# Retention followed by a four-expert feed-forward: one attention visit per chunk in place of three

## The chip, the cores and the metric

The kernel runs on one core of a Trainium2 chip, written in Bass with a Tile layer that places the buffers and their waits; the order of the instructions is the kernel's own. The metric is the device time of one execution in microseconds (us). Engines are called PE (TensorE; its weight loads are a row of their own, PEld), DVE (VectorE), ACT (ScalarE), POOL (GpSimd) and SP (SyncE, which here only issues DMAs).

## The reference, cut to what matters

```python
scores = np.matmul(q, k.transpose(0, 1, 3, 2)) / np.sqrt(64)     # batch 8, heads 8, seq 576, dim 64
ret = scores * Dmat              # Dmat = gamma_h ** (i - j) for i >= j, else 0
x = np.matmul(ret, v)            # -> 4608 tokens x 512
p = domain_probs / (domain_probs.sum(-1, keepdims=True) + 1e-09)
for e in range(4):
    out += p[:, e:e + 1] * (np.maximum(x @ w1[e], 0) @ w2[e])    # 512 -> 1024 -> 512
```

There is no softmax, so a chunk of 128 positions needs its own masked scores and one 64x64 state per head, summed over the chunks before it.

## The kernel before, in words

**The two parts.** Attention makes the token tiles `xT` (512 tokens each, nine of them); the experts turn a tile into 512 x 512 outputs. The weight products run as Strassen's seven in place of eight (`up_fast`, L650, and `Down`, L594), after a classical start (`up_classical`, `downs`, L490 and L512) that lasts until sums of weights and tokens are ready (`weight_sums`, `token_sums`, `down_sums`).

**Stages.** The main loop (L950) goes over pairs of tile and expert, a stage. Each stage has two half-stages g = 0 and 1, one call of `up_fast` each. A half-stage issues four fills (`fill(1)` to `fill(4)`, L971), in each of which the down products of the stage before are put between the up products. In the fast form the PE order of a half-stage is P R V V P Q W V P R W P V W, each letter being four matmuls of 256 columns into the PSUM bank of that name: `upP`, `upQ`, `upR`, `downV`, `downW`. P is written four times. Before the third writing DVE must have read the second (L675), before the fourth DVE must have read the third (L683). Bank Q is read for the last time by ACT at L677, before `fill(2)` ends, and is not used again until ACT copies P into it at L669 in the next half-stage.

**Attention between them.** Batches 0 and 1 are done in the head of the program, batches 2 to 7 by `Chain` (L738). Of a batch there are four chunks of 128 and a remainder of 64. Of each chunk PE has three pieces: `S` (scores, 8 matmuls of 64 rows, L328), `kv` (states, 8 matmuls of 64 columns, L339) and `O` (8 matmuls of 64 columns at L369, and from the second chunk on 4 full ones with the states before it, L372). They go to PSUM banks of the ring `at` (a0, a1, a2). DVE masks the scores (`mask`, L333, two of them) and sums the states (`kv_sum`), POOL copies the states to `sbd` (L362), ACT or DVE copies `O` into `xT` (L242). POOL also multiplies and casts the loaded q, k, v (L279, L281), and SP transposes q and k by DMA (L297). `Chain` keeps a list per engine; `emit` gives out the next entry when the numbers of entries done on other engines are reached. After every fill `between` (L960) offers PE one entry; `sums` and `window` give DVE and ACT theirs. So a batch has 14 PE entries, each between two full products.

**The head.** `plan` and `at(g, ...)` (L846) put small work behind the g-th group of the classical start. Behind groups 26 to 33 stand the sums of w1 of expert 2, behind 51 to 54 the `down_sums` of w2 of expert 1 (L562 to L565). Their result `dsum` lies in the buffer `w2s_1`, which before that holds the loaded k, q, v of chunk 1 of batch 1 (`raw_units`, L92): tags `w2s_0` to `w2s_3` serve as raw buffers for four chunks first. The remainder of batch 1 is transposed by PE (`Trem`, L315).

Of the kernel before, what the change touches and what calls it, by code (L numbers as in the profile page):

```python
# [23 lines left out]
def kernel(  # L24
# [10 lines left out]
    nc = tc.nc  # L35
# [215 lines left out]
    class Att:  # L251
# [111 lines left out]

        def O(self, c):
            st = self.sT[c]
            o = self.o = bank("at", [128, NP, C], FP32, "oc")
            for p in range(NP):
                for j in range(2):
                    nc.tensor.matmul(o[64 * j:64 * j + 64, p, :], lhsT=self.mc("v", c)[:, 2 * p + j, :],  # L369
                                     rhs=st[:, j, p, :], start=(p == 0), stop=False, skip_group_check=True)  # L370
            for p in range(NP if c else 0):
                nc.tensor.matmul(o[:, p, :], lhsT=sbd[:, c - 1, p, :], rhs=self.qc(0, c)[:, p],  # L372
                                 start=False, stop=(p == NP - 1), skip_group_check=True)
# [9 lines left out]
        def Srem_mask(self):  # L383
            st = self.sT["r"] = att2.tile([128, NP, R], BF16, tag="sT", name="sTr")
            nc.vector.tensor_tensor(st, self.srem, trir[:, :].unsqueeze(1).to_broadcast([128, NP, R]), op=MULT)
# [208 lines left out]
    class Down:  # L594
# [7 lines left out]

        def product(self, i):
            hT, h, w, t = hTs[self.nt, self.e], hsum[self.nt, self.e], w2_sb[self.e], dsum[self.e]
            lo, hi, a, b = slice(0, 4), slice(4, 8), slice(0, HD), slice(HD, Dm)
            if i == 1:
                self.V, self.W = (one_bank(x, [128, 2, HD], FP32, "down" + y) for x, y in zip(self.tags, "VW"))
            o, l, r = {1: (self.V[:, 0], hT[:, lo, :HT], w[:, lo, a]),
                       2: (self.V[:, 0], hT[:, hi, :HT], w[:, hi, a]),
                       3: (self.V[:, 1], h.get(4), w[:, hi, b]),  # L610
                       4: (self.W[:, 0], hT[:, hi, HT:], t[:, 2]),
                       5: (self.V[:, 1], h.get(1), t[:, 0]),
                       6: (self.W[:, 0], h.get(2), t[:, 1]),
                       7: (self.W[:, 0], hT[:, lo, HT:], w[:, lo, b])}[i]
            for k in range(NFC // 2):
                nc.tensor.matmul(o, lhsT=l[:, k, self.s * 128:(self.s + 1) * 128], rhs=r[:, k],  # L616
                                 start=(i == 1 and k == 0), stop=(k == NFC // 2 - 1), skip_group_check=True)
# [17 lines left out]
        def out(self, i, halves=(slice(0, 2),)):  # L635
            ns = 2 * i + self.s
            t, po = self.nt * NSUB + ns, (self.V, self.W)[i]
            pe = probs[:, self.e, t:t + 1]
            for x in halves:
                cols = slice(x.start * HD, x.stop * HD)  # L640
                a, src = acc[self.nt][ns][:, cols], po[:, x].rearrange("p a d -> p (a d)")
                if self.e == 0:
                    nc.scalar.activation(a, src, Copy, scale=pe)
                else:
                    nc.vector.scalar_tensor_tensor(a, src, pe, a, op0=MULT, op1=ADD)  # L645
                if self.e == E - 1:
                    eng = nc.scalar if len(halves) == 1 and x.start else nc.sync
                    eng.dma_start(out=out[t * 128:(t + 1) * 128, cols], in_=a)
# [87 lines left out]


    class Chain:  # L738
        def __init__(self):
            self.todo = {k: [] for k in ("PE", "DVE", "ACT", "POOL")}  # L740
            self.done = dict.fromkeys(self.todo, 0)
            self.seen = dict(self.done)
            self.now, self.begun, self.tokens = 0, {}, 2 * S
            for b in range(2, B):
                self.batch(b)

        def batch(self, b):
            A, n = Att.__new__(Att), b - 2
            P, V, X = 14 * n, 13 * n, 5 * n

            def add(kind, f, **need):
                self.todo[kind].append((f, need))

# [11 lines left out]

            g = nc.gpsimd
            for c in range(NCH):
                free = {"PE": P - 14 + (7 if c < 2 else 13)} if n else {}
                if c == 3:
                    free = {"PE": P + 2}  # L770
                if c == 0:
                    add("POOL", lambda: (begin(), cast(A.cast, "k", 0, g)), **free)
                else:
                    add("POOL", lambda c=c: cast(A.cast, "k", c, g), **free)
                add("POOL", lambda c=c: cast(A.cast, "q", c, g))
                add("POOL", lambda c=c: (cast(A.cast, "v", c, g), transposes(c)))
            add("POOL", lambda: cast(A.cast_rem, "k", g), **({"PE": P} if n else {"first": 1}))
            add("POOL", lambda: cast(A.cast_rem, "q", g))
            add("POOL", lambda: (cast(A.cast_rem, "v", g), transposes(NCH)))
            add("POOL", lambda: A.put_krem(g, A.qr[:, 1]), later=(b, NCH))  # L780

            def tokens(c):
                A.x(c, nc.scalar)
                self.tokens = b * S + min((c + 1) * C, S)

            def O(c, v, x):
                add("PE", lambda: A.O(c), DVE=V + v, ACT=X + x)

            def Sc(c, v, x):
                add("PE", lambda: A.S(c), DVE=V + v, ACT=X + x, later=(b, c), **({} if n else {"first": 2}))  # L790

            def kv(c, v, x=0):
                add("PE", lambda: A.kv(c), DVE=V + v, ACT=X + x)

            Sc(0, 0, -1 if n else 0), kv(0, 0), Sc(1, 2, 0), O(0, 3, 0), kv(1, 4), Sc(2, 5, 1), O(1, 6, 0), kv(2, 7)
            Sc(3, 8, 2), O(2, 9, 0), kv(3, 10)
            add("PE", A_(A, "Srem"), DVE=V + 11, later=(b, "r"))
            O(3, 11, 3)
            add("PE", A_(A, "Orem"), DVE=V + 13)
            for c in range(NCH):  # L800
                for j in range(2):
                    add("DVE", lambda c=c, j=j: A.mask(c, j), PE=P + (1, 3, 6, 9)[c])
                add("DVE", lambda c=c: A.kv_sum(c), PE=P + (2, 5, 8, 11)[c])
            add("DVE", A_(A, "Srem_mask"), PE=P + 12)
            for c in range(NCH + 1):
                add("ACT", lambda c=c: tokens(c), PE=P + (4, 7, 10, 13, 14)[c], tile=(b * S + min((c + 1) * C, S) - 1) // NT)

        def emit(self, kind, nt, strict=True):
# [4 lines left out]
            for k, n in need.items():  # L813
                if k == "later":
# [3 lines left out]
                    else:  # L818
                        ok = (b, c) in self.begun and (not strict or self.now >= self.begun[b, c] + 5)
                elif k == "first":  # L820
                    ok = len(rem1) < n
                elif k == "tile":
# [47 lines left out]
    def rem1_casts():  # L870
        for n in "kqv":
            a1().cast_rem(n, nc.gpsimd)
            loads["cast"] += 1
            load_ahead(len(PIECES))

    def a1():
# [16 lines left out]
    def narrow():  # L893
# [5 lines left out]
    at(48, narrow, lambda: state.update(t1=token_sums(1)), lambda: [f() for f in state["t1"][:3]])  # L899
    rem1 = {3: lambda: a1().Trem(), 5: lambda: (a1().Srem(), a1().Srem_mask()),  # L900
            7: lambda: (a1().Orem(), a1().x(NCH, nc.vector))}

# [7 lines left out]
    s0 = sums_at(weight_sums, 0, 20, 21, 22)  # L910
    sums_at(weight_sums, 2, 26, 28, 30, 33)
    sums_at(weight_sums, 3, 36, 38, 49, 50)
    sums_at(down_sums, 1, 51, 52, 53, 54)
    for g in range(49, 56):
        at(g, lambda: pool(1, 1))
# [19 lines left out]
    owed = [((1, 1), (2, 0), s0[3])]  # L935
    for e in (2, 3, 0):

# [12 lines left out]
    for nt, e in [(nt, e) for nt in range(1, n_nt) for e in range(E)][1:]:  # L950
# [9 lines left out]
        def between(i):  # L960
# [3 lines left out]
            if i == 3:  # L964
                pool(nt, 4 if gaps < 8 else 3 - g)
            rem1.pop(gaps, int)()
            chain.emit("PE", nt)
            chain.seen.update(chain.done)
            chain.now += 1

        def fill(i):  # L971
            if not fast:
                for _ in range(4):
# [9 lines left out]
            elif i == 2:  # L983
                d().product(6)
                d().copy("U")
                d().product(2)
            elif i == 3:
                d().product(7)
                d().add(12)
# [11 lines left out]
        def sums(i):  # L1001
# [3 lines left out]
            turns = {(0, 1): 0 if old else 2, (0, 2): 0 if old else 1, (0, 3): 1,  # L1005
                     (1, 1): 2, (1, 2): 1, (1, 3): 0 if new else 1}[g, i]
            if g == 0 and old:
# [5 lines left out]
            for _ in range(turns):  # L1013
                window("DVE")

        def window(kind):
# [7 lines left out]
        while nt not in tsum:  # L1024
            tokens(nt)
            if nt not in tsum:
                moved = [chain.emit(k, nt, strict=False) for k in ("POOL", "PE", "DVE", "ACT")]
                assert any(moved), (nt, chain.done, {k: v[:1] for k, v in chain.todo.items()})
        while front and e == 0:
            front.pop(0)()  # L1030
# [52 lines left out]
```

## Time and profile before

| | |
|---|---|
| median of 4 executions | 529.15 us (528.67 to 529.77) |
| profiled execution | 529.77 us, of which its span is 528.06 us |
| PE busy | 515.3 us, 98% of the span, 4878 matmuls |
| DVE, ACT, POOL busy | 397.4, 303.4, 180.7 us |
| granted PE clock, mean | 0.998 |
| longest idle times ended by a release, PE | 1.6 us in all, twice, waiting for DVE L675 |

Busy time of an engine counts its instructions and not what they hide. Because matmuls overlap, PE's rows are best read by their starts: from the start of one group of four matmuls to the start of the next is what that group costs PE.

### The profile page before, as it was taken

Reading aid. Unit: us, or ns where it says so; the run is one execution under the profiler, and the core shown is the slowest. Engines: PE = TensorE matmul, PEld = TensorE weight load, DVE = VectorE, ACT = ScalarE, POOL = GpSimd, SP = SyncE. Lnnn points to the kernel's source line nnn. Section 1 sums busy time; section 2 is a strip of 40 time slices with the busy share of each in tenths; the row PEclk is TensorE's granted clock in tenths of the full one; section 3 lists DMA queues with packets and bytes.
Section 4 is the critical chain, followed back from the end, with each engine's and each line's share of the span. In section 5 each row is a group of like instructions: output and inputs, shape, how many; then the busy total and the mean of one; then the engine's idle time right before and its main releaser. Section 6 shows DMA issues by size and latency. Waiting matters only on the chain.

```text
span 528.1 us, 12528 instructions
## 1 busy us (share of the span) xinstructions
PE 515.3 (98%) x4878; PEld 400.3 (76%) x4894; DVE 397.4 (75%) x736; ACT 303.4 (57%) x624; POOL 180.7 (34%) x273
## 2 busy tenths in 40 slices
PE   8999999899999999999999999999999999999995
PEld 3644455588666888888888888888888888888884
DVE  5624568888765898788878897788688976886675
ACT  3462254466346555755576666665765666666661
POOL 6702275253433244524424243333424121000010
PEclk9999999999999999999999999999999999999999
DMA  9999999752554239722764149241652110011002
GB/s 236 188 206 202 205 188 201 149 109 45 125 134 102 59 81 151 161 51 46 154 113 101 31 88 215 60 82 25 179 110 42 47 44 1 2 41 41 1 2 80
DMA packets 149260, 54.11 MB, mean 102 GB/s; under 512 B 130732, under 2 KB 144044, under 8 KB 149200
## 3 DMA queue, kind: packets, MB, share of 16 engines
q1 hardware_dynamic: 141872, 44.92, 39.4%
q0 software_dynamic: 7328, 8.39, 9.4%
q8 instruction: 38, 0.62, 0.5%
q14 instruction: 22, 0.18, 0.1%
HBM read 45.16 MB, written 9.44 MB: 103 GB/s over the span
## 4 chain that ended last, share of the span: by engine, by line
PE 92%; DVE 4%; issue 2%; DMA 1%; POOLq 0%; POOL 0%; SPq 0%; DVEq 0%
PE upP L663 21%; PE downV L616 18%; PE downW L616 14%; PE upR L663 10%; PE po L534 9%; PE ph L493 7%; PE upQ L663 5%; PE s L328 2%; PE oc L369 2%; PE kvp L339 1%; PE oc L372 1%; DVE acc L645 1%; DMA raw<-in_q_dram 1%; PE warm_out L164 1%; DVE qm L413 0%
## 5 line engine op out<-in xcount | busy, mean ns | idle before, releaser
L684 POOL TENSOR_SCALAR hT<-hT 128x512 bf16<-128x512 bf16 x62 | 38.3, 618 | 251.0 <-DVE hT L683 248.1
L663 PEld LDWEIGHTS <-wt 128*128 128x128 bf16 x992 | 92.6, 97 | 20.5 <-issue 3.0
L616 PEld LDWEIGHTS <-hT 128*128 128x128 bf16 x928 | 90.8, 98 | 11.4 <-issue 0.8
L663 PEld LDWEIGHTS <-wsum 128*128 128x128 bf16 x744 | 71.1, 98 | 10.0 <-issue 0.7
L663 PE MATMUL upP<-xT,wt 128*128 128x256 bf16 x496 | 74.6, 273 | 1.6 <-DVE upR L675 1.6
L616 PEld LDWEIGHTS <-hsum 128*128 128x128 bf16 x696 | 68.1, 98 | 8.2 <-issue 0.2
L675 DVE TENSOR_TENSOR upR<-upP,m 128x512 f32<-128x512 f32 x62 | 43.3, 698 | 40.9 <-PE upP L663 19.6
L616 PE MATMUL downV<-wt,hT 128*128 128x256 bf16 x464 | 69.3, 273 | 0.4 <-DVE acc L645 0.4
L669 ACT ACTIVATE upQ<-upP 128x512 f32<-128x512 f32 x62 | 36.2, 585 | 45.4 <-PE upP L663 45.3
L686 ACT ACTIVATE hT<-upR 128x512 bf16<-128x512 f32 x62 | 37.0, 597 | 38.6 <-PE upR L663 38.6
L677 ACT ACTIVATE hT<-upQ 128x512 bf16<-128x512 f32 x62 | 37.0, 597 | 32.9 <-PE upQ L663 31.7
L691 ACT ACTIVATE hT<-upP 128x512 bf16<-128x512 f32 x62 | 37.0, 597 | 31.8 <-DVE downW L633 16.0
L534 PE MATMUL po<-wt,hT 128*128 128x512 bf16 x213 | 51.9, 379 | 0.6
L683 DVE TENSOR_TENSOR hT<-upP,m 128x512 bf16<-128x512 f32 x62 | 42.7, 689 | 12.2 <-PE upP L663 9.8
L333 DVE TENSOR_TENSOR sT<-s,tri 128x512 bf16<-128x512 f32 x56 | 37.1, 681 | 5.8 <-PE s L328 5.8
L509 ACT ACTIVATE hT<-ph 128x512 bf16<-128x512 f32 x40 | 23.5, 597 | 29.1 <-PE ph L493 28.2
L663 PE MATMUL upR<-tsum,wsum 128*128 128x256 bf16 x248 | 37.2, 273 | 0.5 <-DVE tsum L562 0.5
L663 PE MATMUL upP<-tsum,wt 128*128 128x256 bf16 x248 | 37.2, 272 | 0.3 <-DVE hT L683 0.3
L663 PE MATMUL upP<-tsum,wsum 128*128 128x256 bf16 x248 | 37.4, 273 | 0.0
L663 PE MATMUL upR<-xT,wsum 128*128 128x256 bf16 x248 | 37.2, 273 | 0.0
L663 PE MATMUL upQ<-xT,wt 128*128 128x256 bf16 x248 | 37.2, 273 | 0.0
L586 DVE TENSOR_TENSOR hsum<-hT 128x512 bf16<-128x512 bf16 x58 | 33.9, 585 | 4.3 <-POOL hT L684 1.2
(134 smaller groups left out, 940.1 us busy)
## 6 DMA issues: line engine op xcount, KB each, us to landing
out_dram<-acc SPq DMA_DIRECT2D x32, 256.0 KB, 2.6
wt<-in_moe_w_dram POOLq DMA_DIRECT2D x6, 1024.0 KB, 25.3
raw_k<-in_k_dram SPq DMA_DIRECT2D x24, 256.0 KB, 3.8
raw_q<-in_q_dram SPq DMA_DIRECT2D x24, 256.0 KB, 3.4
raw_v<-in_v_dram SPq DMA_DIRECT2D x24, 256.0 KB, 3.8
raw<-in_k_dram SPq DMA_DIRECT2D x8, 256.0 KB, 5.7
raw<-in_q_dram SPq DMA_DIRECT2D x8, 256.0 KB, 5.8
raw<-in_v_dram SPq DMA_DIRECT2D x8, 256.0 KB, 5.6
```

The costliest lines, as they stand in the source:

```text
L333: nc.vector.tensor_tensor(self.sT[c][:, j], self.s[c][j], tri[:, :].unsqueeze(1).to_broadcast([128, NP, C]), op=MULT)
L493: nc.tensor.matmul(ph[:, ts], lhsT=w1_sb[e][:, dc, fc * 128:(fc + 1) * 128], rhs=xts[nt][:, dc, ts], start=(dc == 0), stop=(dc == NDC - 1))
L534: nc.tensor.matmul(po, lhsT=hT[:, fc, ns * 128:(ns + 1) * 128], rhs=w2_sb[e][:, fc, d:d + w], start=(fc == 0), stop=(fc == NFC - 1))
L616: nc.tensor.matmul(o, lhsT=l[:, k, self.s * 128:(self.s + 1) * 128], rhs=r[:, k], start=(i == 1 and k == 0), stop=(k == NFC // 2 - 1), ski ...
L663: nc.tensor.matmul(ps[:, l], lhsT=wa(kc)[:, f:f + 128], rhs=xa(kc), start=(start and l == 0 and kc == 0), stop=(kc == 1), skip_group_check ...
L669: nc.scalar.activation(Q, P, Copy)
L675: nc.vector.tensor_tensor(R_, P, m5, op=ADD)
L677: nc.scalar.activation(hT[:, lo, t0], Q, Relu)
L683: nc.vector.tensor_tensor(h22, P, m5, op=ADD)
L684: nc.gpsimd.tensor_scalar(h22, h22, float("inf"), 0.0, op0=MIN, op1=MAX)
L686: nc.scalar.activation(hT[:, lo, t1], R_, Relu)
L691: nc.scalar.activation(hT[:, hi, t0], P, Relu)
```

## The change

Scores of chunk c+1, states of chunk c and output of chunk c become one PE entry, `visit`. It stands only behind `fill(3)` (the entries of a batch's first chunk and its remainder also elsewhere). `O` goes to bank Q, and its copy to `xT` is put at the beginning of `fill(4)` (`put_late`). Of product 2 of `Down` (`downV`) three matmuls stay in front of the third P and one moves behind R, so that the PE order becomes P R V V P Q W V(3) P R V(1) W P V W. The outputs of expert 0 are half moved from ACT to DVE. In the head the `down_sums` of expert 1 go from groups 51 to 54 up to 32 to 35, those of expert 2 take their place, and the last w1 sum of expert 2 goes from 33 to 31. The remainder of batch 1 is transposed by DMA, and its masked scores take the place of its transposed k. The DMA transposes of a chunk are issued behind the cast of q, not behind that of v.

```diff
-        def O(self, c):
+        def O(self, c, tag=None):
             st = self.sT[c]
-            o = self.o = bank("at", [128, NP, C], FP32, "oc")
+            o = self.o = one_bank(tag, [128, NP, C], FP32, "oc") if tag else bank("at", [128, NP, C], FP32, "oc")
...
-            st = self.sT["r"] = att2.tile([128, NP, R], BF16, tag="sT", name="sTr")
+            st = self.sT["r"] = self.qr[:, 1]
...
-        def product(self, i):
+        def product(self, i, part=slice(0, NFC // 2)):
...
-            for k in range(NFC // 2):
+            for k in range(NFC // 2)[part]:
...
-                if self.e == 0:
+                if self.e == 0 and i == 1:
                     nc.scalar.activation(a, src, Copy, scale=pe)
+                elif self.e == 0:
+                    nc.vector.tensor_scalar_mul(a, src, pe)
...
-                add("POOL", lambda c=c: cast(A.cast, "q", c, g))
-                add("POOL", lambda c=c: (cast(A.cast, "v", c, g), transposes(c)))
+                add("POOL", lambda c=c: (cast(A.cast, "q", c, g), transposes(c)))
+                add("POOL", lambda c=c: cast(A.cast, "v", c, g))
...
+        def visit(self, A, b, c, last):
+            add, all_ = self.add, self.all
+            L, l = (A, c - 1) if c else (last, NCH - 1)
+            lb = b if c else b - 1
+            new = A is not None
+            def run():
+                if new:
+                    A.S(c)
+                if L:
+                    L.kv(l)
+                    L.O(l, "Q")
+                    self.late.append(lambda: self.put(L, lb, l))
...
+            if L:
+                add("DVE", lambda: L.kv_sum(l), **done)
+            for j in range(2 if new else 0):
+                add("DVE", lambda j=j: A.mask(c, j), **done)
+            if c == 0:
+                M = L or Later("a1")
+                add("PE", lambda: M.Srem(), DVE=all_["DVE"], later=(lb, "r"), any=1)
+                add("DVE", lambda: M.Srem_mask(), PE=all_["PE"])
+                add("PE", lambda: M.Orem(), DVE=all_["DVE"], any=1)
+                add("ACT", lambda: self.put(M, lb, NCH), PE=all_["PE"], tile=(lb * S + S - 1) // NT)
...
             a1().cast_rem(n, nc.gpsimd)
...
+        a1().dmaT(NCH)
...
-    sums_at(weight_sums, 2, 26, 28, 30, 33)
+    sums_at(weight_sums, 2, 26, 28, 30, 31)
+    sums_at(down_sums, 1, 32, 33, 34, 35)
     sums_at(weight_sums, 3, 36, 38, 49, 50)
-    sums_at(down_sums, 1, 51, 52, 53, 54)
-    for g in range(49, 56):
+    sums_at(down_sums, 2, 51, 52, 53, 54)
+    at(50, lambda: a1().put_krem(nc.gpsimd, a1().qr[:, 1]))
+    for g in range(48, 56):
...
-            rem1.pop(gaps, int)()
-            chain.emit("PE", nt)
+            if i == 3 or chain.todo["PE"] and "any" in chain.todo["PE"][0][1]:
+                chain.emit("PE", nt)
...
         def fill(i):
+            if i == 4:
+                chain.put_late()
...
-                d().product(2)
+                d().product(2, slice(0, 3))
             elif i == 3:
+                d().product(2, slice(3, 4))
                 d().product(7)
```

## The prediction

> **What bounds the kernel now.** I read the page first (busy times, then the shares of the chain that ended last), then PE's rows in the timeline by their starts, then the DVE and POOL timelines of the head.
>
> ```profile
> PE 515.3 (98%) x4878; PEld 400.3 (76%) x4894; DVE 397.4 (75%) x736; ACT 303.4 (57%) x624; POOL 180.7 (34%) x273
> ...
> PE 92%; DVE 4%; issue 2%; DMA 1%; POOLq 0%; POOL 0%; SPq 0%; DVEq 0%
> ```
>
> PE is busy for 98% of the span and carries 92% of the chain. What PE spends on a piece is what the kernel pays, and another engine matters only where PE waits for it. The change removes no product but eight small transposes, so its gain has to be time that PE loses around the pieces. The timeline of a fast stage, about 300 to 313 us:
>
> ```profile
> 301.37 0.60 PE L616 MATMUL downW<-wt,hT 128*128 128x256 bf16 x4
> ...
> 301.90 0.40 PE L328 MATMUL s<-qkT 64*128 64x128 bf16 x8
> ...
> 302.23 0.61 PE L663 MATMUL upP<-tsum,wt 128*128 128x256 bf16 x4
> ...
> 303.11 0.60 PE L616 MATMUL downW<-dsum,hT 128*128 128x256 bf16 x4
> ...
> 303.64 0.41 PE L369 MATMUL oc<-sT,vm 128*64 128x128 bf16 x8
> ...
> 303.99 0.40 PE L372 MATMUL oc<-qkT,sbd 128*128 128x128 bf16 x4
> ...
> 304.22 0.60 PE L663 MATMUL upP<-xT,wt 128*128 128x256 bf16 x4
> ...
> 308.36 0.69 DVE L683 TENSOR_TENSOR hT<-upP,m 128x512 bf16<-128x512 f32 x1 [0.17 <-PE upP L663]
> 308.59 0.60 PE L616 MATMUL downW<-wt,hT 128*128 128x256 bf16 x4
> ...
> 309.10 0.60 PE L663 MATMUL upP<-tsum,wt 128*128 128x256 bf16 x4
> ...
> 311.72 0.60 PE L616 MATMUL downV<-dsum,hsum 128*128 128x256 bf16 x4
> ...
> 312.25 0.32 PE L339 MATMUL kvp<-vm,km 128*64 128x64 bf16 x8
> ...
> 312.49 0.61 PE L663 MATMUL upP<-tsum,wsum 128*128 128x256 bf16 x4
> ```
>
> Undisturbed products start 0.436 us apart (four matmuls at 0.109). Read what stands between a product and the next beyond that: scores 302.23 - 301.37 - 0.436 = 0.42, states 0.33, an output with states 0.67; the product behind a narrow piece runs about 0.014 longer. So a chunk costs PE 0.44 + 0.35 + 0.68 = 1.47 us. Then read the lead: 301.37 to 301.90 is 0.53, 0.09 more than a product needs, and the pieces at 303.64 and 312.25 have the same. It is paid once per piece.
>
> The head has pieces standing together (PE's timeline, 63 to 72 us):
>
> ```profile
> 63.38 3.62 PE L493 MATMUL ph<-xT,wt 128*128 128x512 bf16 x16
> ...
> 68.24 0.40 PE L328 MATMUL s<-qkT 64*128 64x128 bf16 x8
> 68.56 0.32 PE L339 MATMUL kvp<-vm,km 128*64 128x64 bf16 x8
> 68.81 0.82 PE L493 MATMUL ph<-xT,wt 128*128 128x512 bf16 x3
> ...
> 71.42 0.41 PE L369 MATMUL oc<-sT,vm 128*64 128x128 bf16 x8
> 71.67 0.29 PE L339 MATMUL kvp<-vm,km 128*64 128x64 bf16 x8
> ```
>
> **1. The merged visit.** Scores to states 0.32 (68.24 to 68.56). First half of an output to states, both of 64 columns, 0.25 (71.42 to 71.67), against 0.35 from that half to a full matmul (303.64 to 303.99): staying in one shape saves 0.09 to 0.10. States to output isn't in the trace. Upper end: states to a full matmul, 0.25 (68.56 to 68.81). I take 0.16, the 0.25 less the 0.09, because it is the same change of shape left out; a lower end of 0.12 is the 0.22 seen from states at 71.67 to the next product, less 0.10. Sum: lead 0.53, scores 0.32, states 0.16, output 0.35 and 0.23 (303.99 to 304.22) = 1.59; less the 0.436 of the product 1.15 us, against 1.47. Saved 0.32 (0.23 to 0.36). The first chunk, without the full half, saves the same. In the changed order 23 visits hold three pieces, the last holds two (0.2 saved), and the first scores stand alone: 23 x 0.31 + 0.2 = **-7.3** (-5.5 to -8.3). Remainder pieces are full-width already (0.12 and 0.23) and keep their price.
>
> **2. Transposes of batch 1's remainder.** Eight matmuls between products, 0.44 us: **-0.44**. In their place SP issues two transposes, 1.25 to 2.2 us each in SP's rows.
>
> **3. One matmul moved behind R.** 308.59 to 309.10 is 0.51, not 0.44: the fourth P waits until DVE has read the third (308.36 + 0.69 = 309.05). One matmul more in between is 0.109, more than the 0.07 missing. It is seen in 36 half-stages, 2.8 us together, nearly always where no piece stood in that gap: **-2.8** (-2 to -2.8). The price: the third P comes 0.11 earlier against DVE's L675, which starts 0.64 to 0.78 behind the second P in 54 of 62 cases and so ends by 1.48; the third P is due at 15 x 0.109 = 1.64. Cover 0.15 us; nothing is lost while DVE is on time.
>
> **4. Other waits of PE for DVE.** At 94.5 PE waits 1.43 us in the gap (1.6 against even spacing) for L675, behind twelve weight and token sums on DVE. Sums of the same length stay there, but scores and remainder (0.55) now lie inside that wait: -0.7. At 149.4 it waits 0.47 behind a down sum that is gone there: -0.45. Six smaller ones, 0.9 together, mostly where L675 itself came late: half of them, -0.4. Together **-1.5** (0 to -2.5).
>
> **5. The down sums moved up.** Behind group 32 the L562 of expert 1 writes the buffer that held chunk 1 of batch 1, so it must wait until POOL has cast that chunk's v. DVE and POOL rows there:
>
> ```profile
> 59.78 0.75 DVE L524 SCALAR_TENSOR_TENSOR acc<-po,probs,acc 128x512 f32<-128x512 f32 x1 [0.98 <-PE po L534]
> ```
>
> ```profile
> 67.28 0.61 POOL L281 CAST vm<-raw 128x512 bf16<-128x512 f32 x1
> ```
>
> The second row is that cast. Its load landed at 66.98, behind the weights, so no engine can hasten it. In the changed DVE order L562 stands directly ahead of the L524 that now starts at 59.78. DVE is in order: it stands from 58.8 to about 67.8, L562 takes 0.68, that L524 ends near 69.1. PE goes on through the banks it has and then needs the one this L524 empties, for the ph at 63.38. It starts at 69.15: 5.8 us idle. The next two banks are each emptied behind one more down sum, 0.4 and 1.0 late. Scores of chunk 0 stood at 68.24 and now at about 75.5: **+7.3** (+6 to +8.5). POOL's later casts wait for those PE pieces, so the head moves as a whole, and little comes back.
>
> The clock: the windows view shows PE's clock granted at 1.00 up to its last matmul (522.48) and at 0.50 in 526 to 528, and at the start PE's timeline shows four 128-column transposes 0.42 apart at 6.12 and 0.22 apart at 10.69. So PE is slow before work and again 3.5 us behind it, and 5.8 idle us can cost it speed. The rows alone bound that by 0 and 4.6 us, half of the 9.2 us from the first matmul at 1.26 to 10.5, where the start is seen at full pace. I take **+1.0**, near the low end, because DVE paces the groups behind the wait and hides part of a slow PE. The skill has a rule on it that speaks against this change: "TensorE: Matmul & The Clock Gate", Part 1, has the clock halve after an idle window of about 3.4 us and return after as long a busy one. An estimate from that page alone is 1.7 us, half of one window, and a sum of 0.7 more; without the rule it would be 1.0 less.
>
> **6. The rest.** The token sums for tile 2 follow an output copied one half-stage earlier: by ACT's 0.5 spacing and DVE's two accumulations R there waits 1.1 in place of 0.69: **+0.4** (0 to 1). ACT's late copy (0.60) falls between L691 and L669. Counted from the fourth P, L691 starts at 0.63, the copy at 1.13, with expert 0 one scaled output until 2.2, L669 until 2.8; the next P that needs it is due at 3.05. That slack of 0.25 hides it; if it goes, each visit pays what exceeds it. The added DVE output (about 0.7) takes the place of ACT's. POOL keeps its casts, ahead by at least two half-stages. A POOL or SP delay matters first for the scores of batch 2: their second transpose would land near 100, PE comes there at about 100.4; 0 to 1.5 us, taken as 0.
>
> **Sum.** -7.3 - 0.44 - 2.8 - 1.5 + 7.3 + 1.0 + 0.4 = -3.3, so 526.4 for an execution like the profiled one (529.77, span 528.06 and 1.7 around it). That one is the highest of the four; from the median 529.15 the same difference gives 525.8. I say **526.0**.
>
> **Rivals.** (A) *The early down sum does not hold DVE*, because the casts are over by then. Then +8.3 falls away: 518. Against it: the load's landing at 66.98. (B) *Half clock for as long as at the start*: +3.6, 529.6; for it speak 5.8 idle us, against it that PE's work behind the wait is dense. (C, the slower side) *DVE ends each half-stage with a visit*: two accumulations, two masks and L675 then follow each other from 1.05 behind the fourth P; my reckoning ends at 4.39 and the third P needs it at 4.63. Beyond 0.24 us of delay (L586 takes 0.41 alone but 1.25 at 106.46, beside POOL) PE pays the excess; at 0.4 us for 24 visits +9.6: 535.6. (D) *States to output change shape after all and item 4 gives nothing*: +1.8 +1.5: 529.3.
>
> **How the numbers follow.** Forecast 0.55 (own range 524 to 528), A 0.10, B 0.13, C 0.10, D 0.12. Measurement can tell about 0.2%, 1.06 us. Faster takes the forecast and A, 0.65; same the larger part of B and D, 0.18; slower C and their rest, 0.17. The range leaves out A and C, 2 in 10: 522 (items 1, 4 and 5 at their good ends, 1.0, 1.0 and 1.3, and part of the clock) to 531 (B and D, 1.5 more for their spread).
>
> **What would show it.** Item 1: L328, L339, L369 starting 0.32 and 0.12 to 0.25 apart. Item 3: no W to P spacing of 0.51. Item 5: one idle time of PE near 63 to 69, L562 released by POOL's cast of v, and the clock's record behind it. C: L675 later than 1 us behind its P, PE waiting for it. The forecast falls if PE's idle in the head is under 4 or over 10 us, or if PE waits for DVE or ACT in the visits' half-stages.

## The result

The changed kernel takes 527.87 us (median; 527.05 to 529.43) against 529.5 of the kernel before in the same runs (528.14 to 533.04). The ratio is 0.9975 [0.9969, 0.9982], a gain of 1.3 us (the two medians stand 1.6 apart) where the forecast had 3.15 (3.3 by its sum). The sign was right and the time lies in the range, but the forecast's own sum is off by 2 us, more than the gain itself. The profiled execution took 527.83 us, with a span of 526.0.

The first rows to set against those of before are the busy times and the shares of the chain that ended last, on the page of the changed kernel:

```profile
PE 505.9 (96%) x4871; PEld 401.7 (76%) x4886; DVE 405.0 (77%) x744; ACT 297.3 (57%) x613; POOL 181.0 (34%) x275
...
PE 77%; DVE 6%; DMA 6%; SPq 4%; issue 4%; POOL 2%; POOLq 0%; DVEq 0%; ACT 0%
```

PE is busy for 9.4 us less, while the span is 2.1 shorter. The rest went into idle time: PE's share of the chain fell from 92% to 77%, and DMA, SP's queue and POOL, which had next to none, stand in it. So the chain now runs through a load and a cast.

A merged visit, from PE's timeline of the changed kernel (start, duration; read the distances between starts):

```profile
303.30 0.60 PE L616 MATMUL downW<-wt,hT 128*128 128x256 bf16 x4
303.83 0.40 PE L328 MATMUL s<-qkT 64*128 64x128 bf16 x8
304.15 0.32 PE L339 MATMUL kvp<-vm,km 128*64 128x64 bf16 x8
304.30 0.39 PE L369 MATMUL oc<-sT,vm 128*64 128x128 bf16 x8
304.63 0.40 PE L372 MATMUL oc<-qkT,sbd 128*128 128x128 bf16 x4
304.86 0.60 PE L665 MATMUL upP<-tsum,wt 128*128 128x256 bf16 x4
```

Lead 0.53, scores 0.32, states to output 0.15, output 0.33 and 0.23: 1.56, less the product's 0.436 is 1.12 us. The forecast had 1.15, and 0.16 for the one distance that no row of before showed.

The head, in two narrow stretches of the timeline with all engines:

```profile
66.36 0.61 POOL L281 CAST vm<-raw 128x512 bf16<-128x512 f32 x1
...
67.00 0.69 DVE L562 TENSOR_TENSOR dsum<-wt 128x1024 bf16<-128x1024 bf16 x1 [9.81 <-POOL vm L281]
...
67.61 0.74 DVE L524 SCALAR_TENSOR_TENSOR acc<-po,probs,acc 128x512 f32<-128x512 f32 x1
...
68.41 0.58 PE L493 MATMUL ph<-xT,wt 128*128 128x512 bf16 x1 [6.48 <-DVE acc L524]
```

Read it from the cast down: the cast of v ends, the early down sum L562 starts after 9.81 idle us of DVE, the L524 queued behind it empties a bank, and PE starts after 6.48 idle us. This is the chain that item 5 drew, link by link.

**Where the time went.** The start of a profile is no measure of the change: the first remainder output (L392) starts between 59.4 and 61.3 us in the profiles of all these kernels (61.30 in before, 59.69 in after). So the two traces are compared by stretches: the head, from that L392 to the first P of the fast products, and the main loop, from there to the last matmul. In the main loop a piece's price is the distance of the products around it less one matmul (0.109 us, 0.216 with 512 columns), and a wait is what two neighbouring products stand further apart than that.

| stretch, us | before | after | measured | forecast |
|---|---|---|---|---|
| head | 29.57 | 38.87 | +9.3 | +8.3 (item 5) |
| pieces of attention, transposes | 36.44 | 28.62 | -7.8 | -7.7 (items 1, 2) |
| W to P spacings above 0.436 | 2.82 | 0 | -2.8 | -2.8 (item 3) |
| P behind sums (94.5, 149.4) | 2.06 | 0 | -2.1 | -1.15 (item 4) |
| R behind token sums | 0.69 | 2.24 | +1.55 | +0.4 (item 6) |
| small waits for DVE | 0.89 | 2.58 | +1.7 | -0.4 (item 4) |
| main loop, all | 431.34 | 421.79 | -9.55 | -11.7 |

By stretches the change is worth -0.25 us and by the ratio -1.3. The difference lies ahead of the first stretch, where PE's work is the same in both kernels. PE's rows show what differs there: four matmuls of 512 columns stand 0.43 us apart each at 6.5 us in the profile of before, and 0.22 apart at 6.2 us in that of after. So before was profiled with PE at half pace for some 5 us longer. The profiles of e10, e11 and e14 (below) have this late start too, and in these four L392 starts between 60.9 and 61.3 us; in the eleven others it starts between 59.4 and 60.0.

The new wait ends with a load, and that load hardly follows PE's start: v of chunk 1 landed at 66.30 us in after and at 66.98 in before, 0.68 apart, where L392 stands 1.61 apart. So the wait would swallow 0.9 us of a late start that before pays in full. The runs fit this: the ratio gives 0.7 to 1.1 us more than the stretches in all five kernels with the wait (after, e2, e4, e1b, e6), 0.75 in e16, and -0.1 to 0.5 in the eight others. No kernel with the wait was profiled with a late start, so it is not shown directly.

### The profile page after: what moved, and what is told of

Same layout as the page of the kernel before. It is cut to its first block, busy times and chain, and to the rows that moved or that the text cites. A ratio compares the mean times of both kernels' runs of the same rounds, so it can differ in the third digit from the quotient of the medians.

```text
span 526.0 us, 12538 instructions
## 1 busy us (share of the span) xinstructions
PE 505.9 (96%) x4871; PEld 401.7 (76%) x4886; DVE 405.0 (77%) x744; ACT 297.3 (57%) x613; POOL 181.0 (34%) x275
## 4 chain that ended last, share of the span: by engine, by line
PE 77%; DVE 6%; DMA 6%; SPq 4%; issue 4%; POOL 2%; POOLq 0%; DVEq 0%; ACT 0%
PE upP L665 19%; PE downV L616 18%; PE downW L616 12%; PE upR L665 9%; PE po L534 5%; PE upQ L665 5%; SPq L111 4%; PE ph L493 3%; DMA wt<-in_moe_w_dram 2%; DMA raw<-in_k_dram 2%; PE s L328 2%; PE oc L372 1%; PE oc L369 1%; PE kvp L339 1%; DVE acc L647 1%
## 5 line engine op out<-in xcount | busy, mean ns | idle before, releaser
L665 PEld LDWEIGHTS <-wt 128*128 128x128 bf16 x992 | 94.9, 98 | 14.3 <-issue 0.5
L665 PEld LDWEIGHTS <-wsum 128*128 128x128 bf16 x744 | 72.7, 98 | 11.8 <-issue 2.3
L616 PE MATMUL downV<-wt,hT 128*128 128x256 bf16 x464 | 78.4, 272 | 1.3 <-DVE acc L645 0.9
L693 ACT ACTIVATE hT<-upP 128x512 bf16<-128x512 f32 x62 | 37.0, 597 | 52.6 <-PE upP L665 41.1
L677 DVE TENSOR_TENSOR upR<-upP,m 128x512 f32<-128x512 f32 x62 | 43.3, 698 | 30.0 <-PE upP L665 17.4
L493 PE MATMUL ph<-xT,wt 128*128 128x512 bf16 (+3 forms) x175 | 38.3, 373 | 6.6 <-DVE acc L524 6.5
L647 DVE SCALAR_TENSOR_TENSOR acc<-downV,probs,acc 128x512 f32<-128x512 f32 (+1 forms) x48 | 34.4, 723 | 9.5 <-PE downV L616 9.4
L586 DVE TENSOR_TENSOR hsum<-hT 128x512 bf16<-128x512 bf16 x58 | 35.5, 613 | 3.2 <-POOL hT L686 1.5
L673 ACT ACTIVATE m<-upR 128x512 f32<-128x512 f32 x62 | 36.8, 593 | 1.8 <-PE upR L665 1.8
```

The source lines that it names most:

```text
L493: nc.tensor.matmul(ph[:, ts], lhsT=w1_sb[e][:, dc, fc * 128:(fc + 1) * 128], rhs=xts[nt][:, dc, ts], start=(dc == 0), stop=(dc == NDC - 1))
L665: nc.tensor.matmul(ps[:, l], lhsT=wa(kc)[:, f:f + 128], rhs=xa(kc), start=(start and l == 0 and kc == 0), stop=(kc == 1), skip_group_check ...
L677: nc.vector.tensor_tensor(R_, P, m5, op=ADD)
L693: nc.scalar.activation(hT[:, hi, t0], P, Relu)
```

## The experiments

Each kernel ran in five rounds beside the kernel before. The last two columns are the stretches of the profile, as above; the changed kernel stands in the first row.

| kernel | us | ratio to before | head | main loop |
|---|---|---|---|---|
| after | 527.87 | 0.9975 [0.9969, 0.9982] | 38.87 | 421.79 |
| e2 head alone | 536.6 | 1.0144 [1.013, 1.0158] | 38.64 | 430.87 |
| e3 head as before | 519.79 | 0.9826 [0.9812, 0.984] | 29.58 | 422.40 |
| e5 split alone | 527.08 | 0.9961 [0.9948, 0.9973] | 29.58 | 429.59 |
| e9 visits alone | 521.02 | 0.9846 [0.982, 0.9871] | 29.57 | 423.67 |
| e1b buffers swapped | 523.99 | 0.9902 [0.9877, 0.9927] | 35.17 | 421.66 |
| e6 PE kept at work | 529.49 | 1.0006 [0.999, 1.0022] | 38.52 | 423.38 |
| e10 sums later | 519.40 | 0.9816 [0.9803, 0.9829] | 29.57 | 421.71 |
| e4 outputs on ACT | 527.18 | 0.9971 [0.9959, 0.9983] | 38.71 | 421.52 |
| e13 output first | 518.14 | 0.9797 [0.9784, 0.9809] | 29.58 | 421.12 |
| e14 casts later | 520.43 | 0.9847 [0.9821, 0.9874] | 29.57 | 423.13 |
| e11 all token sums first | 520.42 | 0.9826 [0.98, 0.9852] | 29.57 | 422.50 |
| e15 two token sums first | 518.97 | 0.9809 [0.9795, 0.9822] | 29.57 | 421.73 |
| e16 later, output first | 517.82 | 0.9795 [0.9781, 0.9808] | 30.27 | 420.55 |

### The parts by themselves

**e2, the head's move on the kernel before:**

```diff
-    sums_at(weight_sums, 2, 26, 28, 30, 33)
+    sums_at(weight_sums, 2, 26, 28, 30, 31)
+    sums_at(down_sums, 1, 32, 33, 34, 35)
-    sums_at(down_sums, 1, 51, 52, 53, 54)
+    sums_at(down_sums, 2, 51, 52, 53, 54)
-    for e in (2, 3, 0):
+    for e in (3, 0):
```

> The kernel before, with one part of the change alone: the down sums of expert 1 move to groups 32 to 35, those of expert 2 to groups 51 to 54. Theory: DVE stands behind POOL's cast of v of chunk 1 of batch 1, PE is idle for about 6.5 us before the first ph of expert 0 of tile 1 and then runs at half clock for about 5 us, and nothing comes back later: +8 to +9.5 less about 0.5 for the down sum that no longer stands before 149 us, so 536 to 539 against 529.5. Rival 1: the head is bound by the landing of batch 1's loads in any case, so that only the clock's share stays: 530 to 531. Rival 2: the idle time comes back in the main loop, where DVE has less to do: 532 to 534.

Measured +1.44% (+7.4 us by the medians), with +9.1 in the head and -0.5 in the main loop. It lies in the theory's interval, and both rivals fall: what the head loses is not got back.

**e3, the changed kernel with the three places of that diff put back:**

> The changed kernel with the sums in the head where the kernel before has them (expert 1 at groups 51 to 54, expert 2 later, weight sums of expert 2 at 26, 28, 30 and 33). Theory: the wait in the head goes and the gains of the visits stay: 527.9 - 8.5 to 9.5 + 0.5 = 518.5 to 520. Rival: the visits need the early sums, because a down sum of expert 2 in tiles 1 and 2 now falls on DVE beside the visits' own work: the gain of the head is eaten by waits of PE for DVE, 523 to 526.

Measured 519.79: 8.1 us under the changed kernel and 1.7% under the kernel before. The head is at its old 29.58; the main loop pays 0.6 more, since a down sum stands before a P again (0.45 near 138 us). The theory holds. The move of the sums, one part of the change, costs most of what the other parts earn.

**e5, the split of product 2 on the kernel before:**

```diff
-                d().product(2)
+                d().product(2, slice(0, 3))
             elif i == 3:
+                d().product(2, slice(3, 4))
```

> The kernel before, with product 2 of each half-stage split: three of its matmuls ahead of R, one behind it. Theory: the 36 spacings of 0.51 from W to P become 0.44, -2.5 to -2.8, and the third P, 0.11 earlier, does not wait: 526.8 to 527.1 against 529.5. Rival: DVE reads the third bank as late as before and the wait moves to the third P: 528.8 to 529.5.

Measured -0.39%, -2.1 us, and -1.75 in the main loop. All but one of the longer W to P spacings went, 2.6 us, but the other waits rose from 3.65 to 4.39, and the rest (0.1) is spread over the loop. A place where the third P now waits more (0.27 in place of 0.16), in this kernel's timeline:

```profile
358.94 0.69 DVE L592 TENSOR_TENSOR hsum<-hT,hsum 128x1024 bf16<-128x1024 bf16 x1
...
359.55 0.69 DVE L675 TENSOR_TENSOR upR<-upP,m 128x512 f32<-128x512 f32 x1
...
359.69 0.49 PE L616 MATMUL downV<-wt,hT 128*128 128x256 bf16 x3
...
360.30 0.27 PE L663 MATMUL upP<-xT,wt 128*128 128x256 bf16 x1
```

The P should start 3 x 0.109 behind 359.69, at 360.02. It starts at 360.30, behind the end of L675 (360.24), which stood in DVE's queue behind L592. The 0.15 us of cover that item 3 counted are enough where L675 starts on time, and only there. The time lies in the theory's interval, but its "does not wait" does not hold.

**e9, the visits without the split, outputs on ACT, head as before:** in the changed kernel, the places of e2 put back, `d().product(2)` whole again, and `if self.e == 0:` for both outputs.

> The merged visits alone: the changed kernel with the head's sums as before, both outputs of expert 0 on ACT and product 2 of each half-stage unsplit. Theory (the visits save what their spacings say, 7.3, with the transposes 0.44 and the wait near 94 us 1.4; from it goes the new wait of R for the token sums of two tiles, 2.2 in place of 0.7, and some 0.7 of waits for ACT's late copy): 529.3 - 9.1 + 2.2 = 522.4, 521.5 to 523. Rival 1 (nothing but the split and the waits named in the forecast matters): 520.5 to 521. Rival 2 (the visits give half, and the split gives more with them than alone): 524 to 525.5.

Measured 521.02, -1.5%, and -7.67 in the main loop; pieces 28.46 against 36.44. So 8 us come from the visits, as item 1 had it, and the new waits (R for token sums 2.24, expert 0 some 1.4) are there without the split. Beside the visits the split does much the same as alone: without it 30 W to P spacings, 2.19 us, are left, and with it the third P waits 0.25 in place of 0.14 at two places (255.63 and 309.80 in after, and as much in e4). The time lies between the theory's range and rival 1's; the waits, which rival 1 leaves out, speak for the theory.

### The wait in the head

**e1b, the casts' order against the buffer:** chunks 0 and 1 of batch 1 in each other's raw buffers, so that the early sum waits for an earlier cast.

```diff
-            t = wpool.tile([128, 3, H * D], FP32, tag=f"w2s_{x}", name="raw")
+            t = wpool.tile([128, 3, H * D], FP32, tag=f"w2s_{x if b != 1 else (1, 0, 2, 3)[x]}", name="raw")
```

> The changed kernel with the raw loads of batch 1's chunks 0 and 1 in each other's buffers, so that the early down sum waits for the cast of v of chunk 0, which ends 3.3 us earlier in the profile of after (63.67 against 66.97). Theory: PE's idle time at the head shrinks by 3.3 us, to about 3.2, and the half clock behind it shortens or goes: -3.3 to -4.3, so 523.6 to 524.6. Rival (the head is bound by the landing of the last loads of batch 1, and the idle time only moves behind them): 526.5 to 527.9.

Measured 523.99: 3.9 us under the changed kernel, and 3.7 in the head. L562 starts at 63.79 in place of 67.00, and PE's idle time is 3.26 in place of 6.48:

```profile
63.79 0.69 DVE L562 TENSOR_TENSOR dsum<-wt 128x1024 bf16<-128x1024 bf16 x1 [6.59 <-POOL vm L281]
...
65.20 5.41 PE L493 MATMUL ph<-xT,wt 128*128 128x512 bf16 x16 [3.26 <-DVE acc L524]
```

The wait is the buffer's, and the rival (the head is bound by the last loads) falls.

**e6, PE kept at work in the wait:** 28 matmuls of 512 columns more, whose output nobody reads.

```diff
+    def keep_warm():
+        o = one_bank("o1", [128, 512], FP32, "warm_out")
+        for _ in range(28):
+            nc.tensor.matmul(o, lhsT=kbd[:, 0, :], rhs=kbd[:, :, :].rearrange("p a i -> p (a i)"), start=True, stop=True)
+
+    at(35, keep_warm)
```

> The changed kernel with 28 added matmuls of 512 columns, whose output nobody reads, in PE's idle time at the head (28 x 0.216 = 6.0 us of 6.5). They keep TensorE at work, so that the clock stays. Theory: the half clock behind the wait costs only what DVE does not hide, 0.5 to 1.0: 526.9 to 527.4. Rival 1: it costs half of its 5 us, as bound only by PE: 525.4. Rival 2: DVE paces the stretch altogether: 527.7 to 527.9.

It is in no theory's interval: 529.49, 1.6 us slower than the changed kernel. But the profile answers its question. Windows of after and then of e6 (window, length, PE, PEld, DVE, ACT and POOL busy, then the granted clock):

```profile
66.00:70.00 4.00, 1.59 (x4) 0.55 (x4) 3.00 (x5) 0.00 (x0) 3.27 (x5) 0.62 1.23 227
70.00:74.00 4.00, 4.00 (x11) 1.40 (x10) 3.70 (x6) 1.43 (x3) 0.60 (x2) 0.53 1.36 193
```

```profile
66.00:70.00 4.00, 3.01 (x14) 1.20 (x13) 2.38 (x4) 0.00 (x0) 2.66 (x4) 1.00 0.98 207
70.00:74.00 4.00, 2.56 (x12) 1.06 (x11) 3.97 (x7) 1.63 (x3) 1.25 (x2) 1.00 1.09 205
```

The clock falls to 0.62 and 0.53 behind the idle time and stays at 1.00 with PE at work. From the start of the early L562 to the next transposes (L309) it is 67.00 to 74.52 with the low clock and 67.62 to 74.23 without it: 7.52 against 6.61. The low clock costs 0.91 us on the path; the forecast had 1.0. In the windows one also sees why it is so little: with the full clock PE is busy for 2.56 of 4 us and DVE for 3.97. The head as a whole is only 0.36 shorter, since v of chunk 1 was cast later in this run (L562 starts 0.62 later). And 1.6 us were lost at 101.85, where the first scores of batch 2 wait 1.68 for a DMA transpose (in after they start at 100.58, without a wait). SP issues that transpose no later than in after; why it landed later stays open.

The forecast weighed a rule of the Trainium skill here, "TensorE: Matmul & The Clock Gate", Part 1: half clock after an idle window of about 3.4 us, full clock after as long a busy one. These runs agree in kind: half clock behind 6.48 and also behind 3.26, slightly less than the page's window (e1b: 0.60 and 0.54 from 65 to 69 us), none where PE kept working. The 1.7 that was estimated from it was above the 0.91 measured, as it counts PE alone.

**e10, the same sums a little later:**

```diff
-    sums_at(down_sums, 1, 32, 33, 34, 35)
+    sums_at(down_sums, 1, 40, 42, 44, 46)
```

> The changed kernel with the early down sums of expert 1 five to eleven groups later in the head (groups 40, 42, 44 and 46 in place of 32 to 35), where POOL's cast of v of chunk 1 is done. Theory: the idle time in the head, 9.3 us with its half clock, goes altogether, and the wait of 0.45 near 138 us that putting the sums back at groups 51 to 54 brought does not come: 518.5 to 519.5. Rival: in those groups DVE also copies transposes and masks scores, each sum holds one of them up and PE waits there: 521 to 524.

Measured 519.40, in the theory's interval; head 29.57, main loop 421.71, as good as either kernel in either stretch. The sums needed other groups, not another order.

### The waits in the main loop

**What R waits for.** The changed kernel at the end of a half-stage, all engines:

```profile
196.71 0.75 DVE L647 SCALAR_TENSOR_TENSOR acc<-downV,probs,acc 128x512 f32<-128x512 f32 x1 [0.65 <-PE downV L616]
196.77 0.65 ACT L242 ACTIVATE xT<-oc 128x256 bf16<-128x256 f32 x2
...
196.94 0.60 PE L665 MATMUL upP<-xT,wt 128*128 128x256 bf16 x4
...
197.38 0.74 DVE L647 SCALAR_TENSOR_TENSOR acc<-downW,probs,acc 128x512 f32<-128x512 f32 x1
...
198.04 0.41 DVE L562 TENSOR_TENSOR tsum<-xT 128x512 bf16<-128x512 bf16 x1
...
198.50 0.27 PE L665 MATMUL upR<-tsum,wsum 128*128 128x256 bf16 x1 [0.96 <-DVE tsum L562]
```

The late copy of tokens on ACT ends at 197.42, but the token sum L562 stands behind two accumulations and starts at 198.04. R is due at 197.38 and starts at 198.50, 1.12 late. The change also gives DVE one more of `Chain`'s entries in the third fill of a second half-stage (a line of the change that is not shown above), here the sum of states L359 at 195.66; DVE is idle for 0.65 us behind it, so it is not what delays R. The same stands at 142.03, where R was due at 140.91. Item 6 counted one such place at 0.4 more than before. The second is at the start of tile 3: there the kernel before had the tokens' copy early enough for the token sum to run ahead of the accumulations of that half-stage.

**e11, the token sum first:** on e3, the copy directly behind the visit, and the first token sum ahead of the accumulations in every tile.

```diff
-                    self.late.append(lambda: self.put(L, lb, l))
+                    self.put(L, lb, l)
                 d().product(4)
+                tokens(nt + 1)
+                if len(front) == 4:
+                    front.pop(0)()
                 d().out(0)
```

> The kernel of the third run (sums in the head as before the change), with the output's copy on ACT directly behind its visit and the first token sum ahead of the two accumulations of the down product on DVE. Theory: R's two waits of 1.12 us for the token sums of tiles 2 and 3 (131.77 and 188.69 in that run) go: -1.9 to -2.3 from 519.8, so 517.5 to 517.9. Rival: the accumulations, now later, keep the down banks and PE waits for them, or ACT's copy delays the hidden layer behind it in every visit: 519.0 to 521.

Nothing gained: 520.42, and 422.50 in the main loop against e3's 422.40. The two waits of 1.12 are gone, but PE waits elsewhere: 0.85 and 0.25 for P near 134 to 139, 0.62 near 193, 0.53 and 0.47 for V in later tiles, where the early sum had not been needed. The rival holds.

**e15, the same in tiles 1 and 2 alone** (`if nt < 3`, and the copy ahead of L693 in sums(3)):

> The kernel of the third run, with the first token sum ahead of the two accumulations of the down product, and the output's copy on ACT ahead of its last hidden copy, in tile 1 and 2 alone; the other tiles stay as they are. Theory: R's two waits of 1.12 us go and, other than in the run before that moved every token sum, nothing comes in their place: -1.8 to -2.3 from 519.8, so 517.5 to 518.0. Rival: DVE has no time to spare in those half-stages, and the accumulations or the next R sum are late by as much as the token sum was early: 519.0 to 520.0.

Measured 518.97, far from the theory and 0.03 under the rival's interval; -0.7 in the main loop where the theory had 2. The second place again, in this kernel:

```profile
187.93 0.74 DVE L647 SCALAR_TENSOR_TENSOR acc<-downV,probs,acc 128x512 f32<-128x512 f32 x1
...
188.59 0.73 DVE L647 SCALAR_TENSOR_TENSOR acc<-downW,probs,acc 128x512 f32<-128x512 f32 x1
188.67 0.60 PE L665 MATMUL upR<-tsum,wsum 128*128 128x256 bf16 x4
...
191.29 0.49 PE L616 MATMUL downV<-wt,hT 128*128 128x256 bf16 x3
191.50 0.69 DVE L677 TENSOR_TENSOR upR<-upP,m 128x512 f32<-128x512 f32 x1
...
192.24 0.38 PE L665 MATMUL upP<-xT,wt 128*128 128x256 bf16 x2 [0.46 <-DVE upR L677]
```

R is on time at 188.67. But from 187.45 on DVE runs without a pause through two accumulations, three more token sums and two hidden sums, and L677 is late: the third P, due at 191.62, starts at 192.24. Of the 1.12 us, 0.62 came back 3.6 us later. DVE's queue behind a tile's last copy is nearly full; its order mostly chooses where PE waits.

**What V waits for.** Expert 0's output, which the change moved from ACT to DVE; the changed kernel:

```profile
223.21 1.04 POOL L279 TENSOR_TENSOR km<-raw_k,gk 128x512 bf16<-128x512 f32 x1
223.29 1.25 DVE L586 TENSOR_TENSOR hsum<-hT 128x512 bf16<-128x512 bf16 x1
...
224.43 0.60 PE L665 MATMUL upR<-tsum,wsum 128*128 128x256 bf16 x4
224.46 0.74 DVE L645 TENSOR_SCALAR acc<-downV,probs 128x512 f32<-128x512 f32 x1
...
225.25 0.38 PE L616 MATMUL downV<-wt,hT 128*128 128x256 bf16 x2 [0.22 <-DVE acc L645]
...
226.83 0.70 DVE L677 TENSOR_TENSOR upR<-upP,m 128x512 f32<-128x512 f32 x1 [0.31 <-ACT downW L622]
```

V is due at 224.87 and starts at 225.25. L645 could have started at 223.7, when its product was done, but stands behind L586, which takes 1.25 us beside POOL's cast. This is 0.38 us in four tiles.

**e4, both outputs on ACT again:**

```diff
-                if self.e == 0 and i == 1:
+                if self.e == 0:
```

> The changed kernel with both first-half outputs of expert 0 on ACT again, as before the change. Theory: the six waits of the first down product V for DVE's scaled output (0.13 to 0.39 us, 1.85 together) go, and the third P behind them has DVE earlier: -1.5 to -2.3, so 525.6 to 526.4. Rival 1: ACT then ends later than the scores or the next hidden layer need it, PE waits there as long: 527.5 to 528. Rival 2: the waits come from the hidden sum beside POOL and fall on the accumulation in its place; no change.

Measured 527.18, and -0.3 in the main loop. The time lies between the theory and rival 1, 0.3 from the latter; the waits speak for rival 1. In the same four tiles V now waits 0.17 and the next P 0.20, together 0.36 in place of 0.38. The timeline of e4 shows by whom:

```profile
216.90 0.59 ACT L242 ACTIVATE xT<-oc 128x512 bf16<-128x512 f32 x1
...
217.38 0.69 ACT L643 ACTIVATE acc<-downV,probs 128x512 f32<-128x512 f32 x1
...
217.95 0.70 ACT L643 ACTIVATE acc<-downW,probs 128x512 f32<-128x512 f32 x1
...
218.52 0.62 ACT L671 ACTIVATE upQ<-upP 128x512 f32<-128x512 f32 x1
219.03 0.61 ACT L673 ACTIVATE m<-upR 128x512 f32<-128x512 f32 x1
```

The late copy and two outputs follow each other without a pause. So ACT has no room for the second output behind the late copy, and DVE has none in that order.

**e13, on e3, L645 ahead of L586 where expert 0 ends:**

```diff
-                    hidden_sum(nt, e, *a)
+                    if before[1] or not fast or i == 2:
+                        hidden_sum(nt, e, *a)
...
                 d().out(1)
+                if g == 1 and fast and before[1] == 0 and (nt, e) >= begin[e]:
+                    hidden_sum(nt, e, 1, 1)
```

> The kernel of the third run (head as before the change) with DVE's scaled output of expert 0 ahead of the hidden sum that runs beside POOL's cast, in place of behind it. Theory: the four waits of 0.38 us of the first down product for that output go: -1.5 from 519.8, so 518.2 to 518.6. Rival: the hidden sum, still 1.25 us long, then delays the R sum and the third P waits, as it did with the output on ACT: 519.3 to 519.9.

Measured 518.14; main loop -1.28 against e3. The timeline of e13:

```profile
215.23 0.75 DVE L645 TENSOR_SCALAR acc<-downV,probs 128x512 f32<-128x512 f32 x1 [0.62 <-PE downV L616]
...
215.90 1.11 DVE L586 TENSOR_TENSOR hsum<-hT 128x512 bf16<-128x512 bf16 x1
215.90 0.60 PE L665 MATMUL upR<-tsum,wsum 128*128 128x256 bf16 x4
...
216.34 0.49 PE L616 MATMUL downV<-wt,hT 128*128 128x256 bf16 x3
...
218.18 0.69 DVE L677 TENSOR_TENSOR upR<-upP,m 128x512 f32<-128x512 f32 x1
```

V starts 0.44 behind R, on time, and of each 0.38 us only 0.07 is left at a later product. L586 is hardly shorter, but it now uses up a pause: in after L677 came behind 0.31 idle us of DVE (at 226.83), here it comes without one (at 218.18). The theory holds.

**e14, on e3, the casts issued a quarter later** (`if i == 4: pool(...)` for `if i == 3`):

> The kernel of the third run with POOL's casts issued one quarter of a half-stage later, so that they no longer fall on the hidden sum that reads and writes bf16 in SBUF. Theory (a DVE instruction of that kind waits until POOL's instruction beside it ends): the hidden sums of 1.25 us become 0.41, the four waits of 0.38 for the expert-0 output go and nothing else comes: 518.0 to 518.6. Rival: the casts fall on other sums of that kind (two hidden sums, a token sum) and the waits only move: 519.3 to 521.

Measured 520.43 and +0.7 in the main loop: the rival. In this profile 54 of 58 L586 take 0.41 to 0.43 us and 4 take 1.25. In e3, 38 take 0.41 to 0.43, and the 20 beside a POOL instruction take 0.58 (5), 0.80 (4) or 1.25 (11). So the mechanism is as stated. But R, V and P now wait at other places, 6.28 us against 5.46 in all, as here behind one of the four:

```profile
243.90 1.04 POOL L279 TENSOR_TENSOR qm<-raw_q,gq 128x512 bf16<-128x512 f32 x1
...
243.97 1.25 DVE L586 TENSOR_TENSOR hsum<-hT 128x512 bf16<-128x512 bf16 x1
...
245.94 0.27 PE L616 MATMUL downV<-wt,hT 128*128 128x256 bf16 x1 [0.31 <-DVE acc L647]
```

**e16, e10 and e13 together:**

> The changed kernel with the two parts that gave something alone: the early down sums at groups 40 to 46, and DVE's output of expert 0 ahead of the hidden sum. Theory (the two waits have separate causes, so their prices add): from the first product of the main loop to the last matmul 421.7 - 1.3 = 420.4 us, against 431.3 in the kernel before, and nothing lost in the head: 517.4 to 518.2. Rival (the time that DVE spends late in a half-stage is short as a whole, and what one order gives the other takes): 421.2 or more, 518.6 to 519.4.

Measured 517.82, 2% under the kernel before and the lowest median, though not apart from e13 by the intervals. The main loop is at 420.55, as the theory says: the two prices add. The head is 0.7 us longer than e10's. In e16 the first early sum, L562, stands beside POOL's L279 and takes 1.46 us from 68.18 (0.68 in e10); the copy of transposes L311 behind it ends at 69.97, and PE starts the scores at 70.03 after 0.63 idle us.

## Why the prediction was right in sign and wrong in size

1. **The merged visit** (-7.3) was right: -7.8 in the pieces with item 2's transposes, 1.12 us a visit against 1.15. Rival D's change of shape did not occur: 0.15, not 0.25.
2. **The split** (-2.8) was right in what it removes and wrong in that "nothing is lost": DVE is not always on time. Alone it is worth 1.75 in the main loop (e5), beside the visits about 2.0 (2.19 less twice 0.11, e9 against after).
3. **The early sums** (+7.3, clock +1.0) were right in their cause, by e1b, e3 and e10, and 1.0 too small by the stretches: PE idles 6.48, not 5.8. That time is set by a landing and not by PE, and in the profile of after PE came there some 0.9 us earlier against it than in that of before, from which the 5.8 was worked out. The low clock cost 0.91 (e6). The banks behind cost 0.46 and 0.98 in e6, as the 0.4 and 1.0 had it. Rival A fell with the row of L562, rival B with e6.
4. **The steps that failed are two**, both on what DVE can bear at the end of a half-stage. Item 6 counted a late token sum at one tile, +0.4; R waits at two, 1.12 each, +1.55, as the sum stands behind two accumulations on DVE. Item 6 also said that the added output "takes the place of ACT's" and gave it no price, and item 4 took half of the small waits away, -0.4. They came out at +1.7, nearly all of it V's waits for that output, which stands behind a hidden sum of 1.25 us beside POOL; put ahead of that sum (e13) it costs 1.28 us less. The two are 3.2 us off together; 0.9 came back, because the waits at 94.5 and 149.4 went more fully than forecast. So the main loop gained 9.55 us in place of 11.7. That the whole came out 1 us better than the stretches is luck: what the wait in the head seems to swallow of a late start stands in no term of the forecast.
5. **Rival C** had the mechanism, DVE late in the half-stages with a visit, and too high a price (+9.6) at too many places: it comes in four tiles and at two tile starts, not in 24 visits. It was held as a rival with a chance of 0.10, where its smaller form belonged in the sum.

What stays open: the late landing in e6, and a direct look at a late start with the wait in the head.

## What to carry to other kernels

Before an instruction is moved up, look up what last reads the buffer it writes, and when that ends; a few groups later the same move was free (e10). An operation handed to another engine is paid for by what is queued in front of it and behind it there, so count that engine's queue in the very place, at the durations that its rows show beside a busy neighbour. Where an engine works without a pause up to its deadline, another order moves most of the wait and removes little (0.7 of 2.2 us in e15); a pause later in the queue is what makes a new order pay (e13 against e11).

## What the runs showed of the hardware

- A DVE sum of two bf16 operands in SBUF (L586, 128x512) took 0.41 to 0.43 us in the 38 cases without a POOL instruction beside it, in the changed kernel. In the 20 cases that started beside one it took 0.58 to 1.25 (1.25 in 11), the longer the more of POOL's instruction was left, and ended 0.28 us behind it in all 20. L645, which reads PSUM, took 0.74 beside the next L279 (224.22 to 225.44). The Trainium skill, "SBUF — State Buffer", "SBUF: two separate sides", has this as an exclusive lock for the whole instruction, between a DVE operation with two SBUF inputs and a GpSimd one that reads SBUF. The rows agree: the L586 at 223.29 starts 0.08 behind POOL's L279 and ends 0.29 behind its end (224.25).
- At the start of the program four matmuls of 512 columns took 0.43 us each near 6.5 us in four profiles and 0.22 near 6.2 us in eleven, in the same order of work, and the first remainder output came 0.9 to 1.9 us later in the four.
- Half clock came behind 3.26 us of idle PE (e1b) as well as behind 6.48 (after). It cost 0.91 us in the second case, as DVE set the pace.
- Two pieces of attention of one tile shape (states, then the first half of an output) stand 0.15 us apart, where a change of shape takes 0.25 (68.56 to 68.81 in the kernel before).
